# Phase 1's weight pieces: 512 columns in place of 256, one begun every fourth tile

## Chip, cores and metric

The kernel runs on one core of one Trainium2 chip. The metric is the device time of one execution in microseconds, the median of several runs. The engines are named as in the profile: PE (TensorE matmuls), PEld (its weight loads), DVE (VectorE), ACT (ScalarE), POOL (GpSimd), SP (SyncE, which here issues all DMAs).

## What is computed

Attention with a threshold under each row's maximum, then two feed-forward layers on the 2304 tokens:

```python
batch, n_heads, seq, head_dim = (4, 8, 576, 64)
scores = scale * np.matmul(q, k.transpose(0, 1, 3, 2))
thresh = np.max(scores, axis=-1, keepdims=True) - tau
scores = np.where(scores >= thresh, scores, -1000000000.0)
scores = scores - np.max(scores, axis=-1, keepdims=True)
attn = np.exp(scores)
attn = attn / (np.sum(attn, axis=-1, keepdims=True) + 1e-09)
x = np.matmul(attn, v)            # to 2304 tokens of 512
...
g = x @ w_gate                    # 512 to 1536
silu = g * (1.0 / (1.0 + np.exp(-g)))
x = silu * (x @ w_val) @ w_out    # 1536 to 512
...
h = np.maximum(x @ w_in, 0.0)     # 512 to 2048
return h * h @ w_out2             # 2048 to 512
```

The weights come in as float64 (the products of a float32 draw and a float64 scalar); the kernel converts them itself.

## The kernel before

Each matrix product of the feed-forward layers is made of three TensorE products of a rounded part (hi, FP32r) and a remainder (lo): hi by hi, hi by lo, lo by hi. So every operand is split: ACT copies with rounding (`ops.copy`, L48), and DVE or POOL subtracts (`ops.sub`, L56).

*Phase 1* runs attention in 144 tiles of 128 queries (4 batches, 4 pairs of heads, 9 tiles each; the fifth of the nine has queries of both heads). Per tile: `QK` (PE, L583), `RED` the row maximum (DVE, L595), `EXP` (ACT, L601) and the threshold (L603), `MASK` (DVE, L612), `RCP` (L618), `NORM` (POOL, L623), `TR` five transposes (PE, L643), copies of these into `ptf` or `pt`, `AV` the product with the values (PE, L699 in batch 0, L702 later), and the copy of its result into `xF` (ACT L48; DVE L714 adds the second half). Two score buffers, three buffers for `e`. Per pair of heads a load (L424) and small moves (L524), all on SP's one queue.

When a batch is done, its tokens go through the first group of the first feed-forward layer, five slices of 128 hidden columns, as *fill* between attention's tiles: for each half batch `stage_x` splits `xF` into `xs_m`, then per slice gate and value (L220) and, after the five, the output product (`out1`, L265). `work` hands out fill by a credit per tile (`rate`). Batches 0 to 2 are done so; the rest is *phase 2*, which has only feed-forward layers.

*The weights' loader.* `Loader` brings float64 weights in pieces of `PIECE` = 256 columns: one DMA on SP (L122), then seven steps: absolute value of the high words (ACT, L131), four integer steps (DVE: L133 and L135 with one tensor in, L139 and L141 with two, one of them the raw words), the rounded copy (ACT, L48) and the remainder (POOL in phase 1, DVE in phase 2, L56). In phase 1 the raw words and most of the working columns lie in parts of `xF` of the last batch, which nothing uses yet; there are `LIVE` = 3 such buffers. Phase 1 needs 7680 columns, 30 pieces: first those of gate and value by slice, then those of w_out.

What sets the order: in the main loop over tiles `loader.start` is called every `cfg["lev"]` = 2 tiles from tile 8 on, and begins a piece if fewer than `cfg["live"][0]` = 3 have steps ahead of their sixth. `loader.tick(engine)` (named LD, LA, LP) lets the first piece that may go on do one step on that engine; a step on another engine than the last needs a newer `age`, and only `start` advances `age`. `loader.until(f, col)` runs starts and ticks in a loop until slice f is converted up to a column; the fill calls it ahead of each slice. Then a list scheduler places every instruction on its engine's queue by priority (program order with the offsets of `cfg["early0"]` and `cfg["early"]`) and by what it depends on; each engine works its queue in order. The scheduler sees dependences of two accesses by the stretch of memory that each covers.

## Time and profile before

| | us |
|---|---|
| median of 3 runs (1180.57 to 1181.55) | 1181.24 |
| profiled execution | 1181.87 |
| its span, first to last instruction | 1179.8 |
| PE busy | 1142.7 (97%) |
| DVE busy | 874.8 (74%) |
| ACT busy | 647.2 (55%) |
| POOL busy | 294.4 (25%) |

The shares are means over stages of different kinds: POOL works only in phase 1, which ends at about 467 us. So the rows below are by stretch. The profiled execution lies 2.1 us above its span, and 0.6 us above the median.

### The profile page before, as it was taken

How to read it: one execution, taken by the hardware profiler on the slowest of the kernel's cores; microseconds unless marked ns; L12 is line 12 of the kernel's file. 1: busy time of each engine (PE TensorE's matmuls, PEld its weight loads, DVE VectorE, ACT ScalarE, POOL GpSimd, SP SyncE). 2: the span in 40 equal slices, each digit the busy share in tenths (PEclk: the TensorE clock that was granted, in tenths of full speed). 3: DMA queues.
4: the chain of work that ended last, by engine and by line, in shares of the span. 5: the costliest groups of instructions: out<-in, count | busy, mean ns of one | idle time of the engine just before them, and what ended most of it. 6: DMA issues, size and time to landing. Idle time of an engine off the chain costs nothing.

```text
span 1179.8 us, 19121 instructions
## 1 busy us (share of the span) xinstructions
PE 1142.7 (97%) x6564; PEld 1010.0 (86%) x6564; DVE 874.8 (74%) x2058; ACT 647.2 (55%) x1552; POOL 294.4 (25%) x421
## 2 busy tenths in 40 slices
PE   5888899999999999999999999999999999999998
PEld 4677889999999999998888888888888888888887
DVE  6989996799989994789985863468458858755533
ACT  5878888888777774454442432245455525433321
POOL 4556775777766653000000000000000000000000
PEclk9999999999999999999999999999999999999999
DMA  5666533444343310232320210002102101100111
GB/s 170 167 175 177 148 91 81 100 117 106 91 104 94 97 32 1 81 100 80 88 65 8 83 54 1 1 27 67 50 19 71 55 19 36 55 1 1 45 58 59
DMA packets 40848, 84.73 MB, mean 72 GB/s; under 512 B 5936, under 2 KB 6960, under 8 KB 40752
## 3 DMA queue, kind: packets, MB, share of 16 engines
q1 hardware_dynamic: 40752, 83.52, 25.2%
q8 instruction: 52, 0.85, 0.3%
q14 instruction: 44, 0.36, 0.1%
HBM read 52.23 MB, written 4.72 MB: 48 GB/s over the span
## 4 chain that ended last, share of the span: by engine, by line
PE 81%; DVE 11%; issue 3%; ACT 2%; DMA 1%; POOL 1%; SPq 0%; POOLq 0%; DVEq 0%; ACTq 0%
PE mm L220 34%; PE mm L311 17%; PE mm L265 9%; PE s L583 4%; PE bank L220 4%; PE bank L643 4%; PE bank L265 4%; PE bank L702 3%; DVE e L612 3%; DVE nm L595 2%; PE bank L699 1%; DVE xs_m L56 1%; DMA xF<-in_w_dram 1%; DVE pt L56 1%; DVE xF L714 1%
## 5 line engine op out<-in xcount | busy, mean ns | idle before, releaser
L220 PE MATMUL mm<-xs,wa 128*128 128x512 f32 (+2 forms) x1152 | 226.3, 356 | 0.5 <-ACT x L48 0.5
L220 PEld LDWEIGHTS mm<-xs,wa 128*128 128x128 f32 x1152 | 193.4, 188 | 30.9 <-ACT x L48 0.7
L220 PE MATMUL mm<-xs,wb 128*128 128x512 f32 (+1 forms) x840 | 175.5, 368 | 0.0
L643 PE MATMUL bank<-ident,e 128*128 128x128 f32 x720 | 163.6, 276 | 6.9 <-ACT x L48 3.6
L220 PEld LDWEIGHTS mm<-xs,wb 128*128 128x128 f32 x840 | 146.8, 188 | 26.4
L623 POOL TENSOR_SCALAR e<-e,r 128x576 f32<-128x576 f32 x144 | 113.9, 792 | 87.0 <-DVE r L618 39.2
L612 DVE SCALAR_TENSOR_TENSOR e<-s,thr,e 128x577 f32<-128x577 f32 x144 | 116.8, 812 | 14.7 <-ACT e L601 11.0
L595 DVE TENSOR_REDUCE nm<-s 128x1 f32<-128x576 f32 x144 | 108.0, 751 | 7.7 <-PE s L583 6.8
L663 ACT ACTIVATE pt<-bank 128x384 fp32r<-128x384 f32 (+1 forms) x216 | 92.2, 437 | 38.5 <-PE bank L643 33.2
L220 PE MATMUL bank<-xs_m,wa 128*128 128x288 f32 x576 | 109.7, 326 | 3.0 <-DVE xs_m L56 1.9
L601 ACT ACTIVATE e<-s,nm 128x576 f32<-128x576 f32 x144 | 107.1, 744 | 7.2 <-DVE nm L595 3.9
L643 PEld LDWEIGHTS bank<-ident,e 128*128 128x128 f32 x720 | 97.4, 142 | 15.7 <-POOL e L623 4.9
L294 ACT ACTIVATE k_th<-mm 128x512 f32<-128x512 f32 (+1 forms) x80 | 43.7, 547 | 120.0 <-PE mm L220 118.9
L583 PE MATMUL s<-kh,qs 128*128 128x288 f32 x256 | 80.7, 329 | 16.2 <-DVE e L612 8.8
L702 PE MATMUL bank<-pt,vs 128*128 128x256 f32 (+1 forms) x480 | 92.9, 321 | 2.2 <-POOL pt L56 1.5
L220 PEld LDWEIGHTS bank<-xs_m,wa 128*128 128x128 f32 x576 | 89.0, 189 | 5.8 <-DVE xs_m L56 3.3
L295 DVE TENSOR_TENSOR k_th<-k_th 128x512 f32<-128x512 f32 (+1 forms) x80 | 50.7, 634 | 52.6 <-ACT k_th L294 52.0
L131 ACT ACTIVATE wf<-wr 128x256 f32<-128x256 f32 x106 | 45.5, 433 | 72.3 <-DMA wr<-in_w_dram 57.1
L702 PEld LDWEIGHTS bank<-pt,vs 128*128 128x128 f32 x480 | 73.6, 189 | 4.3 <-POOL pt L56 2.8
L324 DVE TENSOR_TENSOR xF<-xF,mm 128x512 f32<-128x512 f32 x54 | 37.0, 684 | 54.2 <-PE mm L311 54.2
L583 PE MATMUL s<-kl,qs 128*128 128x288 f32 x256 | 73.9, 302 | 0.0
L583 PEld LDWEIGHTS s<-kh,qs 128*128 128x128 f32 x256 | 49.5, 194 | 22.4 <-DVE e L612 13.3
(125 smaller groups left out, 2280.4 us busy)
## 6 DMA issues: line engine op xcount, KB each, us to landing
wr<-in_w_dram SPq DMA_DIRECT2D x106, 256.0 KB, 3.0
raw<-in_qkv_dram SPq DMA_DIRECT2D x15, 896.0 KB, 4.6
kh<-land SPq DMA_DIRECT2D x60, 144.0 KB, 2.5
kl<-raw SPq DMA_DIRECT2D x60, 144.0 KB, 2.7
xF<-in_w_dram SPq DMA_DIRECT2D x30, 256.0 KB, 3.1
out_dram<-xF SPq DMA_DIRECT2D x18, 256.0 KB, 2.0
qs<-land SPq DMA_DIRECT2D x30, 144.0 KB, 2.5
qs<-raw SPq DMA_DIRECT2D x30, 144.0 KB, 2.6
```

Of the source, the lines that this page charges most:

```text
L220: mm(pt[:, :n], w[:, a, col + c * P : col + (c + 1) * P], xs[:, b, c, :], start=(i == 0), stop=(i == len(TERMS) - 1),)
L265: mm(pt[:, :n], w[:, a, 2 * DM + m * P : 2 * DM + (m + 1) * P], u[:, b, :], start=(k == 0), stop=(k == last),)
L295: ("D", lambda: nc.vector.tensor_tensor(th, th, th, op=ALU.mult)),
L311: mm(pt, u[:, b, s * P : (s + 1) * P], w[:, a, DM : 2 * DM], start=(k == 0), stop=(k == last),)
L583: mm(sp[:, cols], l, r[:, cols], start=(n_ == 0), stop=(n_ == len(pairs) - 1),)
L595: nc.vector.tensor_reduce(nm, sv, axis=AX.X, op=ALU.max, negate=True)
L601: nc.scalar.activation(e[:, :S], st[t]["s"][:, :S], AF.Exp, bias=st[t]["nm"])
L612: nc.vector.scalar_tensor_tensor(e, st[t]["s"][:, : S + 1], st[t]["thr"], e, op0=ALU.is_ge, op1=ALU.mult, accum_out=sum_)
L623: nc.gpsimd.tensor_scalar(e, e, scalar1=r, scalar2=1.0, op0=ALU.mult, op1=ALU.mult)
L643: mm(dst[:, j], e[:, c0 : c0 + P], ident, is_transpose=True, start=(j == 0), stop=(j == len(cols) - 1),)
L663: nc.scalar.activation(pt[:, s0 : s0 + n, o : o + P], src, AF.Copy)
L702: mm(o[:, :n], hd["vs"][:, SLOT[k % 5], :], pt[:, k, lo : lo + n], start=(k == 0), stop=(k == 9))
```

## The change

In phase 1 a piece has 512 columns, 15 pieces in place of 30. `PIECE` is now a pair, one size for each phase; phase 2 keeps 256 columns, and its loads and steps cover the same memory as before. There are two buffers for three: the raw words lie in two row blocks of `xF`, the last batch's first 512 columns of each (`two` gives loads and steps two rows of half a piece), the working columns in the third batch's part. `start` is called every fourth tile (`lev` 4), two pieces are live at once, and two of the four calls of `tick` for DVE are gone from the loop. An assertion says that the loader is done before batch 2 writes its part.

```diff
--- before.py
+++ after.py
@@ -29,8 +29,8 @@
 G2 = [4, 4, 4, 4]
 NBS = [(0, 512), (512, 512), (1024, 512), (1536, 512), (2048, 256)]
 NB = 512
-PIECE = 256
-LIVE = 3
+
+PIECE = (512, 256)
 VW = 5 * D
 RAWW = 2 * S + 2 * VW
 
@@ -108,24 +108,25 @@
 
         def add(self, src, f, width, area, k):
             w = area[:, k * 2 * width : (k + 1) * 2 * width].rearrange("p (a c) -> p a c", a=2)
-            self.todo += [(src, f, w, c0) for c0 in range(0, width, PIECE)]
+            self.todo += [(src, f, w, c0, PIECE[self.phase]) for c0 in range(0, width, PIECE[self.phase])]
             return w
 
         def start(self):
             self.age += 1
             if not self.todo or sum(x[2] < 6 for x in self.live) >= cfg["live"][self.phase]:
                 return
-            src, f, w, c0 = self.todo.pop(0)
+            src, f, w, c0, n = self.todo.pop(0)
             self.n += 1
-            sl = slice(c0, c0 + PIECE)
+            sl = slice(c0, c0 + n)
             raw, fl = self.bufs[self.n % len(self.bufs)]
-            nc.sync.dma_start(raw, src[f, :, sl])
-            g = self.steps(raw, fl, w[:, 0, sl], w[:, 1, sl], self.n)
+            two = lambda x: x.rearrange("p (a n) -> p a n", a=2)
+            nc.sync.dma_start(raw.bitcast(I64), two(src[f, :, sl]))
+            g = self.steps(raw, two(fl), two(w[:, 0, sl]), two(w[:, 1, sl]), self.n)
             self.live.append([g, next(g), 1, "S", self.age, (f, c0)])
 
         def steps(self, raw, fl, whi, wlo, n):
-            words = raw.bitcast(I32).rearrange("p (n two) -> p n two", two=2)
-            lo, hi = words[:, :, 0], words[:, :, 1]
+            words = raw.bitcast(I32).rearrange("p a (n two) -> p a n two", two=2)
+            lo, hi = words[:, :, :, 0], words[:, :, :, 1]
             yield "A"
             it = fl.bitcast(I32)
             nc.scalar.activation(fl, hi.bitcast(F32), AF.Abs)
@@ -382,10 +383,8 @@
     up = p1.enter_context(tc.tile_pool(name="up", bufs=1))
     xsp = p1.enter_context(tc.tile_pool(name="xsp", bufs=1))
 
-    for j in range(LIVE):
-        c0 = LAST + j * PIECE
-        fl = xF[:, LIVE, c0 : c0 + PIECE] if c0 + PIECE <= NT else up.tile([P, PIECE], F32, name=f"wf{j}")
-        loader.bufs.append((xF[:, j, LAST : LAST + 2 * PIECE].bitcast(I64), fl))
+    for j in range(2):
+        loader.bufs.append((xF[:, 2 * j : 2 * j + 2, LAST : LAST + PIECE[0]], xF[:, j, LAST - S : LAST - S + PIECE[0]]))
     psum = p1.enter_context(tc.tile_pool(name="psum", bufs=1, space=PSUM))
     bank = [psum.tile([P, 512], F32, name=f"bank{j}") for j in range(4)]
     mp1 = Mm(bank[3:])
@@ -704,6 +703,8 @@
         out_x = [(xF[mr, p, base + dst : base + dst + w], slice(src, src + w)) for dst, src, w in segs]
 
         def main():
+
+            assert b < 2 or not loader.todo and not loader.live
             for x_, sl in out_x:
                 ops.copy("A" if not one else cfg["om"], x_, o[mr, sl])
             if one:
@@ -839,7 +840,6 @@
         if 0 <= i - 1 < NTILE:
             at_(RCP, i - 1)
             at_(NORM, i - 1)
-        at_(loader.tick, "D", name="LD")
         at_(mp1.flush, "A", name="FA")
         if i + 1 < NTILE:
             at_(QK, i + 1)
@@ -862,7 +862,6 @@
                 if k == 2:
                     steps = pair_steps(pr + 1)
                 at_(next, steps, name="PS")
-        at_(loader.tick, "D", name="LD")
     while avq or not fstate["end"]:
         mp1.age += 1
         mp1.flush()
@@ -894,7 +893,7 @@
 
     wrp = p2.enter_context(tc.tile_pool(name="wrp", bufs=1))
     loader.bufs = [
-        (wrp.tile([P, PIECE], I64, name=f"wr{j}"), wrp.tile([P, PIECE], F32, name=f"wf2{j}")) for j in range(2)
+        (wrp.tile([P, 2, PIECE[1]], F32, name=f"wr{j}"), wrp.tile([P, PIECE[1]], F32, name=f"wf2{j}")) for j in range(2)
     ]
     wts[0] = W
     loader.phase = 1
@@ -1045,7 +1044,7 @@
     "qs": "A",
     "thr": "A",
     "wl": "PD",
-    "live": (3, 2),
+    "live": (2, 2),
     "fill": 6,
     "om": "A",
     "early0": {
@@ -1053,7 +1052,7 @@
         "RED": -12, "RCP": 4, "MASK": 4, "NEG": -60,
     },
     "three": 20,
-    "lev": 2,
+    "lev": 4,
     "ldat": 8,
     "early": {
         "TR": 8, "LD": -21, "FD": 4, "NEG": -4, "FA": -19, "PL": -12, "PS": -25, "PH": 6, "LS": 64, "RCP": -8,
```

The first place is DVE's queue around tiles 9 and 10 (`nm9` is the row maximum of tile 9, `wf` and `xF` are pieces' working columns). Before:

```order
L595 TENSOR_REDUCE nm9_373<-s1_110 128x1
L141 SCALAR_TENSOR_TENSOR xF_64<-xF_64 128x256
L133 TENSOR_SCALAR wf2_80<-wf2_80 128x256
L595 TENSOR_REDUCE nm10_410<-s0_109 128x1
L612 SCALAR_TENSOR_TENSOR e0_97,sum9_405<-s1_110,thr9_374,e0_97 128x577
L135 TENSOR_SCALAR wf2_80<-wf2_80 128x256
L618 RECIPROCAL r9_406<-sum9_405 128x1
L139 SCALAR_TENSOR_TENSOR wf2_80<-xF_64,wf2_80 128x256
L141 SCALAR_TENSOR_TENSOR wf2_80<-xF_64,wf2_80 128x256
L612 SCALAR_TENSOR_TENSOR e1_98,sum10_430<-s0_109,thr10_411,e1_98 128x577
L618 RECIPROCAL r10_431<-sum10_430 128x1
```

Now:

```order
L594 TENSOR_REDUCE nm9_372<-s1_109 128x1
L617 RECIPROCAL r8_368<-sum8_367 128x1
L594 TENSOR_REDUCE nm10_408<-s0_108 128x1
L611 SCALAR_TENSOR_TENSOR e0_96,sum9_403<-s1_109,thr9_373,e0_96 128x577
L617 RECIPROCAL r9_404<-sum9_403 128x1
L611 SCALAR_TENSOR_TENSOR e1_97,sum10_427<-s0_108,thr10_409,e1_97 128x577
L617 RECIPROCAL r10_428<-sum10_427 128x1
L594 TENSOR_REDUCE nm11_432<-s1_109 128x1
L594 TENSOR_REDUCE nm12_462<-s0_108 128x1
```

The steps of pieces have left this place: the next one after tile 5 stands behind the row maximum of tile 15.

The second place is where the fill's first output product stands, PE's queue behind the scores of tile 59 before and of tile 61 now (`m00_2_u` is the hidden slice 2, `bank3` and `bank2` are accumulators). Before:

```order
L583 MATMUL s1_110<-kl13_2142,qs13_2140 128x288
L702 MATMUL bank2_86<-pt_132,vs12_2092 128x256 x10
L265 MATMUL bank3_87<-m00_0_u_1351,wa_69 128x288 x3
L265 MATMUL bank3_87<-m00_1_u_1451,wa_69 128x288 x3
L265 MATMUL bank3_87<-m00_2_u_1596,wa_69 128x288
L643 MATMUL bank0_84<-ident_113,e2_99 128x128
L265 MATMUL bank3_87<-m00_2_u_1596,wa_69 128x288
L643 MATMUL bank0_84<-ident_113,e2_99 128x128
```

Now:

```order
L582 MATMUL s1_109<-kl13_2049,qs13_2047 128x288
L266 MATMUL bank3_86<-m00_2_u_1519,wa_69 128x288 x3
L266 MATMUL bank3_86<-m00_3_u_1681,wa_69 128x288 x3
L701 MATMUL bank2_85<-pt_131,vs11_1629 128x256 x8
L266 MATMUL bank3_86<-m00_4_u_1826,wx_73 128x288 x2
L701 MATMUL bank2_85<-pt_131,vs11_1629 128x256
L266 MATMUL bank3_86<-m00_4_u_1826,wx_73 128x288
L701 MATMUL bank2_85<-pt_131,vs11_1629 128x256
L672 MATMUL bank0_83<-pt_131,nident_117 128x384
L672 MATMUL bank1_84<-pt_131,nident_117 128x256
L266 MATMUL bank3_86<-m00_0_u_1272,wa_69 128x288 x3
```

Before, transposes of attention stand between the output's matmuls, and tile 60's scores follow; now the whole first output product and value products of earlier tiles stand in a row, and tile 62's scores behind them. On DVE there, before:

```order
L612 SCALAR_TENSOR_TENSOR e2_99,sum59_2432<-s1_110,thr59_2396,e2_99 128x577
L595 TENSOR_REDUCE nm60_2439<-s0_109 128x1
L618 RECIPROCAL r59_2433<-sum59_2432 128x1
L56 TENSOR_TENSOR pt_132<-bank1_85,pt_132 128x2x128
L595 TENSOR_REDUCE nm61_2480<-s1_110 128x1
L612 SCALAR_TENSOR_TENSOR e0_97,sum60_2473<-s0_109,thr60_2440,e0_97 128x577
L618 RECIPROCAL r60_2474<-sum60_2473 128x1
L56 TENSOR_TENSOR pt_132<-bank0_84,pt_132 128x3x128
```

and now:

```order
L594 TENSOR_REDUCE nm61_2359<-s1_109 128x1
L134 TENSOR_SCALAR xF_64<-xF_64 128x512
L136 TENSOR_SCALAR xF_64<-xF_64 128x512
L140 SCALAR_TENSOR_TENSOR xF_64<-xF_64 128x512
L142 SCALAR_TENSOR_TENSOR xF_64<-xF_64 128x512
L134 TENSOR_SCALAR xF_64<-xF_64 128x512
L715 TENSOR_TENSOR xF_64<-xF_64,bank2_85 64x256
L136 TENSOR_SCALAR xF_64<-xF_64 128x512
L140 SCALAR_TENSOR_TENSOR xF_64<-xF_64 128x512
L142 SCALAR_TENSOR_TENSOR xF_64<-xF_64 128x512
L715 TENSOR_TENSOR xF_64<-xF_64,bank2_85 64x256 x2
```

The two last pieces are converted between the row maximum of tile 61 and the mask of tile 60.

The third place is ACT's queue with the semaphores that its instructions wait for (DMAHW: a DMA's; the others an engine's), near tile 23 before and near tile 31 now, where `xF` is staged into `xs_m` and an attention output goes into `xF`. Before:

```order
L603 ACTIVATE thr22_779<-nm22_778,tau_n_61 128x1
L603 ACTIVATE thr23_812<-nm23_811,tau_n_61 128x1 [waits DVE_49]
L131 ACTIVATE wf2_80<-xF_64 128x256 [waits DMAHW5_49,Pool_49]
L48 ACTIVATE xs_m00_1341<-xF_64 128x288
L601 ACTIVATE e2_99<-s1_110,nm23_811 128x576 [waits PE_49]
L48 ACTIVATE x2_65<-bank1_85 128x2x128
L48 ACTIVATE xF_64<-bank2_86 64x256 [waits PE_49]
```

Now:

```order
L48 ACTIVATE xs_m00_1262<-xF_64 128x288 [waits DMAHW3_49]
L48 ACTIVATE xs_m00_1262<-xF_64 128x288 [waits Activation_49]
L48 ACTIVATE x2_65<-bank0_83 128x3x128 [waits PE_49]
L600 ACTIVATE e1_97<-s1_109,nm31_1007 128x576 [waits DVE_49,PE_49,Pool_49]
L602 ACTIVATE thr31_1008<-nm31_1007,tau_n_61 128x1
L48 ACTIVATE x2_65<-bank1_84 128x2x128
L602 ACTIVATE thr32_1037<-nm32_1036,tau_n_61 128x1 [waits DVE_49]
L600 ACTIVATE e2_98<-s0_108,nm32_1036 128x576 [waits PE_49,Pool_49]
L48 ACTIVATE x2_65<-bank1_84 128x2x128
L48 ACTIVATE xF_64<-bank2_85 64x256 [waits DMAHW1_49,PE_49]
L48 ACTIVATE x2_65<-bank0_83 128x3x128 [waits DVE_49,PE_49]
```

One staging copy and one output copy now wait for a DMA; before neither did.

## Rows read from the trace of the kernel before

**Rows 1.** Busy us by stretch: PE, PEld, DVE, ACT, POOL, then PEclk, DMA, GB/s

```profile
11.40:110.20 98.80, 84.62 (x466) 69.28 (x466) 90.23 (x230) 78.07 (x200) 53.35 (x73) 0.98 0.58 153
110.20:166.30 56.10, 50.41 (x349) 45.66 (x348) 54.81 (x129) 47.03 (x125) 40.47 (x54) 1.00 0.52 139
166.30:195.50 29.20, 28.48 (x209) 26.93 (x209) 22.61 (x55) 23.37 (x62) 18.33 (x26) 1.00 0.38 94
195.50:200.70 5.20, 5.20 (x43) 5.20 (x42) 3.27 (x10) 4.13 (x12) 2.46 (x3) 1.00 0.00 0
200.70:467.50 266.80, 263.90 (x2001) 257.48 (x2001) 233.12 (x570) 204.04 (x524) 173.66 (x245) 1.00 0.35 85
467.50:1179.80 712.30, 707.80 (x3498) 603.50 (x3497) 467.64 (x1063) 287.17 (x628) 0.98 (x2) 1.00 0.14 46
```

**Rows 2.** Line 595 by stretch: count, ns min/median/max, first and last start, shapes

```profile
L595 DVE TENSOR_REDUCE nm<-s x9: 742/757/758, 11.4 to 30.2; 128x1 f32<-128x576 f32 x9
...
L595 DVE TENSOR_REDUCE nm<-s x37: 730/745/758, 11.4 to 110.2; 128x1 f32<-128x576 f32 x37
...
L595 DVE TENSOR_REDUCE nm<-s x16: 737/746/757, 110.2 to 164.2; 128x1 f32<-128x576 f32 x16
...
L595 DVE TENSOR_REDUCE nm<-s x8: 745/752/760, 166.3 to 190.9; 128x1 f32<-128x576 f32 x8
...
L595 DVE TENSOR_REDUCE nm<-s x10: 745/752/760, 166.3 to 198.0; 128x1 f32<-128x576 f32 x10
```

**Rows 3.** DVE groups, 520 to 1179 us: count, busy us, mean ns, idle before

```profile
L295 DVE TENSOR_TENSOR k_th<-k_th 128x512 f32<-128x512 f32 x64 | 44.0, 687 | 40.1 <-ACT k_th L294 39.5
...
L141 DVE SCALAR_TENSOR_TENSOR wf<-wr,wf 128x256 int32<-128x256 int32 x91 | 38.4, 421 | 1.8
...
L135 DVE TENSOR_SCALAR wf<-wf 128x256 int32<-128x256 int32 x91 | 26.4, 290 | 1.9
```

**Rows 4.** Timeline of DVE at 57 us: start, duration, instruction

```profile
57.14 0.29 DVE L135 TENSOR_SCALAR xF<-xF 128x256 int32<-128x256 int32 x1
57.34 0.88 DVE L141 SCALAR_TENSOR_TENSOR wf<-xF,wf 128x256 int32<-128x256 int32 x1
```

**Rows 5.** DVE groups, 11.4 to 110.2 us, then 110.2 to 166.3 us

```profile
L139 DVE SCALAR_TENSOR_TENSOR xF<-xF 128x256 int32<-128x256 int32 x13 | 6.2, 485 | 0.0
...
L535 DVE SCALAR_TENSOR_TENSOR raw<-raw,qscale,land 128x576 fp32r<-128x576 f32 x4 | 4.0, 998 | 2.0 <-ACT land L529 2.0
...
L135 DVE TENSOR_SCALAR wf<-wf 128x256 int32<-128x256 int32 x6 | 2.4, 392 | 0.0
...
L135 DVE TENSOR_SCALAR xF<-xF 128x256 int32<-128x256 int32 x7 | 4.2, 605 | 0.1
...
L133 DVE TENSOR_SCALAR wf<-wf 128x256 f32<-128x256 f32 x4 | 1.6, 398 | 0.0
```

**Rows 6.** Timeline of DVE and of POOL at 139 us

```profile
139.37 0.97 DVE L139 SCALAR_TENSOR_TENSOR xF<-xF 128x256 int32<-128x256 int32 x1
...
139.26 0.81 POOL L56 TENSOR_TENSOR m_u<-m_th,m_u 128x288 fp32r<-128x288 f32 x1
```

**Rows 7.** Line 122, the weights' loads

```profile
DMA to landing us min/median/max: 2.5/3.0/7.5
```

**Rows 8.** Groups: ACT, 520 to 1179 us; POOL, 11.4 to 200.7 us

```profile
L48 ACT ACTIVATE ub<-k_th 128x512 fp32r<-128x512 f32 x47 | 29.6, 630 | 28.6 <-DVE k_th L295 17.4 <-DVE k_th L250 10.9
...
L56 POOL TENSOR_TENSOR wa<-xF,wa 128x256 fp32r<-128x256 f32 x17 | 12.9, 766 | 4.7 <-ACT wa L48 4.6
...
L56 POOL TENSOR_TENSOR pt<-tf,pt 128x384 fp32r<-128x384 f32 x5 | 5.1, 1012 | 0.2 <-ACT tf L666 0.2
```

**Rows 9.** The chain that ended last, at 190 us: start, us, what

```profile
190.36 1.19 PE bank L702 x10
191.55 0.93 PE bank L265 x7
```

**Rows 10.** Timeline of PE at 96 us

```profile
96.64 0.71 PE L643 MATMUL bank<-ident,e 128*128 128x128 f32 x5
```

## The prediction

> **What bounds the kernel now.** I read four views in this order: busy time by stretch, the groups of VectorE's (DVE's) instructions, the timeline, the chain of work. By stretch [rows 1] TensorE (PE) is busy for 707.8 of 712.3 us after 467.5, and for 263.9 of 266.8 us between 200.7 and 467.5. The built order of phase 2 is the same in both kernels, and that of phase 1 is the same on every engine from about tile 62 on. So from 200.7 us on a change in the start time is carried to the end one to one, and all is decided ahead of that. There attention's tiles are counted by their row maximum (L595) [rows 2]: tiles 0 to 35 take 11.4 to 110.2 us (stretch A), 36 to 51 to 166.3 (B), 52 to 61 to 200.7 (C). In A and B DVE is the busiest engine, 90.2 of 98.8 and 54.8 of 56.1 us. In C PE is: 28.5 of 29.2, then 5.2 of 5.2. The weights' conversion is what loads DVE in A and B and is nearly absent in C.
>
> **Price of one conversion instruction on DVE.** A piece has four: two with one SBUF tensor in (L133, L135), two with two (L139, L141). Alone (late in the program, where GpSimd does nothing) they last 290 and 421 ns at 256 columns [rows 3]. At 512 columns an instruction with two inputs lasts 687 ns [rows 3]. One with a single input and 512 columns isn't in the trace: between 290 (no dearer) and 580 (twice); I take 420, since 256 columns add 267 ns with two inputs and the single-input form is faster per column. An instruction begins some 0.08 us before the record of the one ahead of it ends: one of 0.29 us at 57.14 is followed at 57.34 [rows 4]. So one costs on average (290+421)/2 - 80 = 275 ns of DVE's time at 256 columns and (420+687)/2 - 80 = 473 ns at 512.
>
> In A and B they are dearer. In A the eight groups hold 75 instructions and 33.2 us, 443 ns each; in B 43 and 23.4 us, 544 ns each (first and last group in [rows 5]): 0.09 and 0.19 us above the 355 ns alone. The surplus is a collision: at 139.37 an L139 took 0.97 us and ended 0.27 us after the GpSimd instruction that began at 139.26 and lasted 0.81 [rows 6]. I take the surplus per instruction, not per column, as it ends with the other engine's instruction: 0.56 us each in A, 0.66 in B and C. The Trainium skill's page SBUF — State Buffer (Who interferes with whom) says that the two engines' shared port pair is an exclusive lock, held for a whole instruction. By that rule half as many instructions meet half as many locks, and the row agrees.
>
> **Part by part.** The built order tells where the 60 instructions (15 pieces by four) that replace 120 stand: 16 in A, 23 in B, 21 in C; before it was 75, 43 and 2. Pieces are not only wider but later: the hand-over of a piece from one engine to the next needs a newer `age`, which only `start` advances, and that is now called every fourth tile; and only two are begun at a time. Before the fill's weights are used, `until` then forces what is missing.
>
> *A.* DVE loses 75 x 0.36 = 27.2 us and gets 16 x 0.56 = 9.0: -18.2. Then PE (84.6 busy) and ScalarE (78.1, of which some 8 goes too) are late next, so the gain lies between 0 and 18.2. The nearest row is the pace of the first eight tiles, 11.4 to 30.2 [rows 2]: 2.35 us each, with seven 256-wide conversions among them, some 2 us, which is 9 us in 36 tiles, just what is left in A. 36 x 2.35 = 84.6: **-14.2**.
>
> *B.* 43 x 0.46 - 23 x 0.66 = -4.7 on DVE. PE, at 50.4 busy of 56.1, leaves room for that, but the conversions now come in bursts: between -4.7 and +2 (a burst of four at 0.66 that nothing covers), I take **-3.5**.
>
> *New waits.* The raw buffer was one run of columns in one row block of `xF`; now it is a block of two, and what lies between them counts as covered. In the built order a staging copy of `xF` (L48, into xs_m) and a copy of an attention output into `xF` wait for a DMA's semaphore; before none did. Behind such a copy on ScalarE stands the next tile's exp. A load of 256 KB lands 3.0 us after its issue, at most 7.5 [rows 7]; it is 512 KB now. Two such waits stand on ScalarE late in A, one on DVE there and one on DVE in C: 0 if the load is early, up to some 6 us; **+2**. SP's queue gets 15 loads for 30, each waiting for a buffer that frees two pieces earlier; the pair's moves behind them are asked for no earlier than by the order, so I cost them at nothing; an uncovered wait is like the 2.0 us that L535 waited in A [rows 5].
>
> *C.* The three last pieces (columns of w_out) are converted here, after the tiles 52 to 55 have run without any fill. In tiles 52 to 59 DVE had 22.6 us of work in 29.2; 13 conversions at 0.66 (8.6) replace two (0.6): 30.6, about 1 us more than now. Then, at tile 61, DVE does the last two pieces in a row, and PE's queue holds the five w_out groups that read them. From the end of piece 12: two row maxima (0.75 each), piece 13's four steps (1.9), a wait for piece 14's load (some 1), its four (1.9), ScalarE's rounding (0.63), GpSimd's remainder; that is 766 ns at 256 columns and 1012 at 384, so some 1.25 at 512 [rows 8]: 8 us, in which PE has four scores (0.5), two groups (0.8) and eight value matmuls (1.0). After it PE has 37 matmuls of the output, 12 of the next gate, ten value matmuls, ten transposes: 49 x 0.131 + 1.2 + 1.4 + 0.5 = 9.5 [rows 9, 10]. 17.5 us in place of 5.2: +12.3. With the 1 us it is 13.3 at most; if ScalarE and GpSimd are quicker to turn, or PE takes up the value matmuls earlier, half of the 8 us is hidden, so between +7 and +16; I take **+12**. The Trainium skill (Perfetto Trace Analysis, Optimizing Scalar/DVE Operations) says that where Scalar and Vector aren't saturated but hold others up, smaller instructions let work be done sooner. In C that speaks against this change; split in 256 columns, each of the last chain's steps would hand over its first half sooner, by some 2 us in all, an estimate.
>
> Sum: -14.2 - 3.5 + 2 + 12 = -3.7. On the profiled execution of 1181.87 us it gives 1178.2; the median of the runs is 0.6 lower, so **1178 us**. A measurement of this kernel can tell some 0.2% (2.4 us) from no change.
>
> **Rivals.**
> - *The starved fill wins (slower).* If C and the new waits together cost more than the 17.7 us that A and B give, the kernel is slower. With C at +16, the waits at +5 and A at -12, B at -3: +6, 1187 us. For it: PE has no fill for four tiles, and every wait in C falls on the engine that sets the end there [rows 1]. Against it: PE's work up to tile 62 is the same, and A has 14.2 us of idle PE.
> - *The burst hides (much faster).* A falls by 17, C costs 7: -12, 1169 us. For it: DVE is idle for 8.5 us of C now. Against it: PE's queue is in order, and the value matmuls stand behind the output's.
> - *Wide instructions collide in proportion.* If the surplus grows with the columns, B and C's price is 0.473 x 0.464/0.275 = 0.80 us, 0.14 more for 44: +6 on the forecast, 1183 to 1184 us, so little or nothing is left. Against it is [rows 6].
>
> **How the numbers follow.** Forecast 0.40 (of it 0.27 faster by over 0.2%, 0.13 within); starved fill 0.33 (0.30 slower, 0.03 within); hidden burst 0.13; proportional collisions 0.14 (0.09 within, 0.05 slower). Faster 0.40, within 0.25, slower 0.35. The forecast's own range is 1174 to 1182. For 8 in 10 it reaches into both neighbours: A -18 and C +9 give 1168, A -7, C +14 and the waits +4 give 1190.
>
> **What would show it.** Right: tile 36's row maximum begins by about 96 us, DVE's L140/L142 last about 0.69 us where GpSimd is idle, and tile 62's comes at about 197, after a gap of some 17 us from tile 60's. From there to the end both traces take the same 979 us. Wrong: a pace in A that stays near 2.7 us a tile; PE idle at the output's matmuls for much more or less than 6 us; ScalarE waiting for DMAs ahead of xs_m.

## The result

| | before | after |
|---|---|---|
| median of 4 runs each, us | 1180.99 (1180.57 to 1181.55) | 1192.66 (1191.65 to 1196.66) |
| ratio, 95% interval | | 1.0113 (1.0099 to 1.0126) |
| profiled execution, its span | 1181.87, 1179.8 | 1196.66, 1194.9 |
| tile 0's row maximum begins | 11.4 | 9.9 |
| tile 36's | 110.2 | 101.6 |
| tile 52's | 166.3 | 154.8 |
| tile 60's | 195.5 | 190.5 |
| tile 62's | 200.7 | 215.4 |

The change made the kernel 11.7 us slower, where 1178 us (1168 to 1190) was forecast. The profiled execution is the slowest of its four, 4.0 us above their median, so what it shows is larger by that than the usual run; the seventh experiment shows where most of those 4 us may lie.

Busy time by stretch, cut at the same tiles as [rows 1] (PE, PEld, DVE, ACT, POOL, then PEclk, DMA share, GB/s):

```profile
9.90:101.60 91.70, 82.56 (x465) 68.72 (x466) 74.07 (x171) 70.96 (x171) 45.76 (x61) 0.96 0.57 151
101.60:154.80 53.20, 49.25 (x346) 45.05 (x345) 49.23 (x106) 45.11 (x114) 40.40 (x47) 1.00 0.54 143
154.80:190.50 35.70, 25.16 (x148) 20.89 (x147) 29.42 (x63) 23.64 (x59) 21.65 (x26) 0.93 0.45 121
190.50:215.40 24.90, 19.59 (x108) 17.52 (x108) 10.87 (x21) 10.68 (x25) 7.65 (x8) 0.68 0.07 21
215.40:482.50 267.10, 264.06 (x2000) 257.54 (x1999) 233.16 (x570) 203.96 (x524) 173.30 (x245) 1.00 0.35 85
482.50:1194.90 712.40, 707.77 (x3499) 603.93 (x3497) 467.22 (x1063) 287.49 (x628) 1.07 (x2) 1.00 0.15 46
```

From tile 62 on the two traces last 979.1 (before) and 979.5 us (after). Ahead of it, the changed kernel is 11.6 us early at tile 52 (A gave 8.6, B 3.0) and 14.7 us late at tile 62. So ten tiles, stretch C, took 60.6 us in place of 34.4: 26.2 us lost, against 12 in the forecast. In C no engine is full now: PE is busy for 44.8 of 60.6 us, DVE for 40.3. And the column PEclk says 0.93 and 0.68 where [rows 1] have 1.00.

### The profile page after: what moved, and what is told of

Same layout as the page of the kernel before. It is cut to its first block, busy times and chain, and to the rows that moved or that the text cites. A ratio compares the mean times of both kernels' runs of the same rounds, so it can differ in the third digit from the quotient of the medians.

```text
span 1194.9 us, 19005 instructions
## 1 busy us (share of the span) xinstructions
PE 1150.7 (96%) x6564; PEld 1015.6 (85%) x6564; DVE 866.8 (73%) x1998; ACT 644.8 (54%) x1522; POOL 293.6 (25%) x406
## 4 chain that ended last, share of the span: by engine, by line
PE 83%; DVE 7%; ACT 3%; DMA 3%; issue 2%; POOL 2%; SPq 0%; POOLq 0%; DVEq 0%; ACTq 0%
PE mm L221 34%; PE mm L312 16%; PE mm L266 9%; PE bank L221 5%; PE s L582 5%; PE bank L642 4%; PE bank L266 4%; PE bank L701 4%; PE bank L698 2%; DVE e L611 2%; DMA xF<-in_w_dram 1%; DVE nm L594 1%; DMA raw<-in_qkv_dram 1%; DVE pt L56 1%; ACT e L600 1%
## 5 line engine op out<-in xcount | busy, mean ns | idle before, releaser
L221 PEld LDWEIGHTS mm<-xs,wa 128*128 128x128 f32 x1152 | 193.5, 189 | 30.8 <-ACT x L48 0.7
L642 PE MATMUL bank<-ident,e 128*128 128x128 f32 x720 | 159.2, 278 | 10.6 <-ACT x L48 3.7
L296 DVE TENSOR_TENSOR k_th<-k_th 128x512 f32<-128x512 f32 (+1 forms) x80 | 50.8, 635 | 51.3 <-ACT k_th L295 50.8
L132 ACT ACTIVATE wf<-wr 128x256 f32<-128x256 f32 x106 | 45.4, 432 | 71.2 <-DMA wr<-in_w_dram 62.9
L325 DVE TENSOR_TENSOR xF<-xF,mm 128x512 f32<-128x512 f32 x54 | 37.0, 686 | 53.7 <-PE mm L312 53.7
```

What stands on the lines that cost most here:

```text
L221: mm(pt[:, :n], w[:, a, col + c * P : col + (c + 1) * P], xs[:, b, c, :], start=(i == 0), stop=(i == len(TERMS) - 1),)
L296: ("D", lambda: nc.vector.tensor_tensor(th, th, th, op=ALU.mult)),
L642: mm(dst[:, j], e[:, c0 : c0 + P], ident, is_transpose=True, start=(j == 0), stop=(j == len(cols) - 1),)
```

## The experiments

Each kernel ran beside the kernel before. "Conversions" are DVE's instructions of pieces in A, B and C as the built order has them; tile 36 is the time of its row maximum, B and C the lengths of tiles 36 to 51 and 52 to 61, all from the profiled execution.

| kernel | conversions | tile 36 | B | C | median us | ratio (95%) |
|---|---|---|---|---|---|---|
| before | 75, 43, 2 | 110.2 | 56.1 | 34.4 | 1180.99 | |
| after | 16, 23, 21 | 101.6 | 53.2 | 60.6 | 1192.66 | 1.0113 |
| 1: one row block | 41, 19, 0 | 105.8 | 52.2 | 34.9 | 1176.16 | 0.9961 (0.9946, 0.9975) |
| 2: start every 2nd tile | 34, 22, 4 | 105.9 | 59.2 | 36.1 | 1182.34 | 1.0019 (1.0007, 1.0030) |
| 3: before, in two row blocks | 65, 31, 24 | 106.5 | 58.7 | 50.8 | 1197.60 | 1.0145 (1.0120, 1.0170) |
| 4: 1 and 2 together | 47, 13, 0 | 107.2 | 51.2 | 34.9 | 1173.02 | 0.9933 (0.9914, 0.9952) |
| 5: working columns moved out | 24, 20, 16 | 103.8 | 53.7 | 45.3 | 1186.61 | 1.0051 (1.0035, 1.0067) |
| 6: before, start every 4th | 69, 44, 7 | 108.5 | 57.4 | 35.5 | 1182.86 | 1.0026 (1.0015, 1.0037) |
| 7: extra matmuls | 16, 23, 21 | 97.9 | 53.0 | 60.0 | 1194.02 | 1.0116 (1.0101, 1.0131) |
| 8: three buffers | 49, 11, 0 | 109.5 | 53.2 | 34.9 | 1178.59 | 0.9986 (0.9975, 0.9996) |
| 9: 5 and 2 together | 38, 22, 0 | 109.1 | 55.6 | 33.0 | 1178.05 | 0.9984 (0.9972, 0.9995) |
| 10: 4, first start at tile 4 | 47, 13, 0 | 111.1 | 50.6 | 34.8 | 1177.98 | 0.9984 (0.9973, 0.9996) |
| 11: 1, start every 3rd tile | 45, 15, 0 | 107.2 | 51.0 | 34.8 | 1176.06 | 0.9964 (0.9950, 0.9979) |
| 12: 4 again | 47, 13, 0 | 107.7 | 50.8 | 34.8 | 1172.72 | 0.9924 (0.9910, 0.9938) |

(Where an expectation below names other counts by a few, the table's are right.)

Two theories stood against each other on why the pieces come so late. *Pace*: a start only every fourth tile and two live pieces, as the prediction had it. *Block shape*: the raw words now lie in two row blocks of `xF`, and the scheduler takes such a block as one stretch of memory, from the first row block's last batch to the second's. All of the second row block's earlier columns lie in it: attention's results of batches 0 to 2, what `stage_x` reads, and, for the first buffer, the second buffer's working columns.

**1. One row block.** Same width, same starts; only where the buffers lie.

```diff
-        loader.bufs.append((xF[:, 2 * j : 2 * j + 2, LAST : LAST + PIECE[0]], xF[:, j, LAST - S : LAST - S + PIECE[0]]))
+        r0 = LAST - S
+        loader.bufs.append(
+            (
+                xF[:, j, r0 : r0 + 2 * PIECE[0]].rearrange("p (a n) -> p a n", a=2),
+                xF[:, 2 + j, r0 : r0 + PIECE[0]],
+            )
+        )
```

> The changed kernel with the raw words of a piece in one row block of xF (1024 columns, from the third batch's part on) and the working columns in the two row blocks behind; a start still stands at every fourth tile, two pieces live, 512 columns. Theory 'block shape' (the two-row block counts as covering what lies between its two parts, so a piece cannot be placed ahead of attention's copies into xF): all 60 conversions now stand ahead of tile 52 (41 in A, 19 in B), tiles 52 to 61 take 34 us as in the kernel before and the gain of A and B stays: 8 to 10 us, 1169 to 1174 us. Theory 'pace' (every fourth tile and two live make the pieces late): C keeps some 20 of its 26 us, 1185 us or more.

Stretches A, B and C (to tile 60, then to 62), columns as above:

```profile
9.50:105.80 96.30, 80.81 (x466) 65.96 (x466) 86.87 (x194) 77.15 (x184) 54.67 (x66) 1.00 0.62 172
105.80:158.00 52.20, 49.33 (x344) 45.17 (x344) 47.76 (x105) 44.24 (x112) 39.63 (x48) 1.00 0.51 135
158.00:187.60 29.60, 28.85 (x213) 27.47 (x212) 22.46 (x53) 23.84 (x63) 16.86 (x25) 1.00 0.38 92
187.60:192.90 5.30, 5.30 (x43) 5.30 (x43) 3.29 (x11) 4.29 (x12) 2.51 (x4) 1.00 0.00 0
```

C is back at 34.9 us with PE full, and the clock at 1.00 throughout. 1176.16 us: 16.5 less than after, with the pace untouched. So the pace alone doesn't make the pieces late. (In columns it had not changed: 512 every fourth tile for 256 every second.)

**2. A start every second tile**, the two-row block kept.

```diff
-    "lev": 4,
+    "lev": 2,
```

> The changed kernel with a start every second tile in place of every fourth; two-row blocks stay. In its order 34 conversions stand in A, 22 in B, 4 in C. Both theories expect C near 34 to 38 us. 'Block shape' expects that waits for DMAs on ScalarE stay, so some 2 us more than with one block: 1171 to 1177 us. 'Pace' expects all the loss to go, as with nothing else wrong: 1169 to 1172 us.

C is nearly restored (36.1), yet the time is 1182.34: B takes 59.2 us, 3.1 more than before, though DVE is busy for 49.4 us of it in place of 54.8. Twice the columns per tile nearly undo the lateness, but not the other costs of the block. PE's clock falls too, to a mean of 0.97 in B and 0.95 in C. What ScalarE, and then GpSimd, waited for (us in total, times, longest):

```profile
ACT xF L132 <- POOL wa L56: 6.4, 5, 3.2
...
ACT xF L132 <- POOL wx L56: 1.5, 1, 1.5
```

```profile
POOL wa L56 <- DMA xF<-in_w_dram: 2.7, 3, 1.5
```

GpSimd's wait is the mark of the block. Its remainder reads a piece's working columns and its rounded part, no raw words; here it waits for a *load* of raw words. That is the next piece's load into the first buffer, in whose stretch the second buffer's working columns lie. ScalarE's `L132` of a later piece waits for that remainder, and attention's copies and exp stand behind it. The longest of ScalarE's waits (3.2 us, at 151) isn't explained by that alone: GpSimd did other work there and waited for no load, with the remainder late in its queue. That the block put it there is likely, since none of these waits is left in experiment 9, but not shown; experiment 6, without such a block, has a wait of this kind of 3.1 us.

**3. The kernel before, in two row blocks.** 256 columns, three live, a start every second tile as before; only the buffers' places differ: two raw buffers of three are folded, the third lies elsewhere in one row block, and the first buffer's working columns lie in the second's stretch, as a neighbour's do in the changed kernel (in that kernel's writing, with `PIECE` = (256, 256), the two ticks back):

```diff
...
-        loader.bufs.append((xF[:, j, LAST : LAST + 2 * PIECE].bitcast(I64), fl))
...
+        r0, c0 = ((0, LAST), (2, LAST), (0, LAST + PIECE[0]))[j]
+        fl = (xF[:, 2, LAST + 256 : LAST + 512], xF[:, 3, LAST + 256 : LAST + 512], None)[j]
...
+        raw = xF[:, r0 : r0 + 2, c0 : c0 + 256]
+        if j == 2:
+            raw = xF[:, 2, LAST - S : LAST - S + 512].rearrange("p (a n) -> p a n", a=2)
+        loader.bufs.append((raw, fl))
```

> The kernel before with 256 columns, a start every second tile and three live as it was, but two of the three raw buffers laid over two row blocks (256 columns of each) and the third in one row block elsewhere. 'Block shape': pieces are late again (24 conversions in C, output products in a lump behind tile 61 in its order), C takes 15 to 25 us more, A and B lose up to 5: 1190 to 1205 us. 'Pace': 1180 to 1184 us, since the pace is that of before.

1197.60 us, 17 more than before: the block, with a neighbour's columns in it, lengthens C at 256 columns and the old pace too, by 16.4 us. With experiment 1 this is the cause from both sides.

**4 and 12. One row block and a start every second tile**, both edits above in one kernel.

> One row block and a start every second tile: 47 conversions in A, 12 in B and 1 in C's first tile, none in the rest. If DVE's saved time in A and B is what is left, it stands within 3 us of the run with one block and every fourth tile; earlier pieces put 6 more of them into A (some 3 us of DVE there) and 7 fewer into B: 1168 to 1175 us. If late pieces were still costing something in the run with one block, this one is the faster by over 2 us.

> The kernel with one row block and a start every second tile once more, on another chip's time and in five rounds, since the four kernels with one row block lay between 1173.0 and 1178.0. If its gain is the build's (no wait of ScalarE for GpSimd ahead of L132, PE without a fall of its clock in A): 1172 to 1175 us again. If the first 1173.0 was a lucky draw among falls of the clock in A: 1175 to 1178 us.

1173.02 and, some time later, 1172.72 us: 0.7% under the kernel before, the best of all, and it came out twice.

**5. The working columns out of the block.** Raw words stay in two row blocks; the second buffer's working columns go from row block 1 to row block 2, ahead of the second buffer's stretch.

```diff
-xF[:, j, LAST - S : LAST - S + PIECE[0]]
+xF[:, 2 * j, LAST - S : LAST - S + PIECE[0]]
```

> The changed kernel, raw words still in two row blocks and a start every fourth tile, but the second buffer's working columns moved from row block 1 to row block 2: out of the stretch that the first buffer's raw words count as covering. In its order C holds 16 conversions in place of 21, the last behind tile 57 in place of 61, and 22 in A in place of 16. Theory 'pieces hold each other up' (the second buffer's columns lie inside the first's block): most of C's loss goes, 1178 to 1184 us. Theory 'attention's copies hold pieces up' (the blocks cover columns that copies and staging touch): C keeps over half of its 26 us, 1187 to 1193 us.

Tiles 52 to 59 and 60 to 61:

```profile
157.50:197.00 39.50, 32.33 (x207) 29.17 (x207) 31.84 (x70) 27.57 (x71) 25.62 (x30) 0.91 0.41 112
197.00:202.80 5.80, 5.80 (x47) 5.80 (x46) 3.28 (x8) 4.41 (x12) 2.17 (x4) 1.00 0.00 0
```

The second part of C is normal (5.8 us), the first takes 39.5 in place of 29.2. C is 15.3 us shorter than in after and still 10.9 longer than before. So pieces holding each other up are a real part of the loss, and what the fold still covers, attention's copies and staging, is the likely rest. How large each is stays open: the two profiles say 15.3 of 26.2 us of C, but after's lies 4.0 us above its median and this one 3.0 below; the medians say 6.1 (1186.61 for 1192.66) of the 16.5 that one row block gives. The time lies between the two expectations.

**6. The pace alone.** The kernel before with `"lev": 4`.

> The kernel before with one number changed: a start every fourth tile in place of every second (256 columns, one row block each, three live). In its order 89 conversions stand in A and the first eighth of B... 69 in A, 44 in B, 7 in C (75, 43 and 2 before). Theory 'pace': pieces come half as often, the fill starves, 1190 us or more. Theory 'block shape': the scheduler places forced pieces early enough when nothing in memory speaks against it; C costs 3 us more at most: 1179 to 1184 us.

1182.86 us, +0.26%. At half the pace in columns, with one row block, the pieces still come early: 7 conversions in C, C 1.1 us longer.

**7. Extra matmuls in the waits.** The changed kernel with matmuls of a zero tile in the first output product's accumulation.

```diff
...
+                extra = warm.get((nm, m, k // 3), 0)
+                for i in range(extra):
+                    mm(pt[:, :n], zero, us[-1][:, 0, :], start=(k + i == 0), stop=False)
...
```

> The changed kernel with 48 extra matmuls of a zero weight tile (16 ahead of the first output product, 24 ahead of its fourth slice, 8 ahead of its fifth), which add zero; 6.3 us of PE at the full clock. They stand on PE where it waited between 184 and 197 us. Theory 'clock' (some 4 to 6 us of C are PE's work at half its clock after those waits): the granted clock stays near 1.0 in more of 180 to 206 us, tile 62 comes no later than in the changed kernel and up to 4 us earlier, 1188 to 1193 us. Theory 'waits alone': the clock is no cause, and what of the 6.3 us doesn't fit into the waits is added: 1193 to 1199 us.

A, B, C to tile 60, and to 62:

```profile
9.70:97.90 88.20, 79.39 (x465) 66.41 (x466) 74.18 (x172) 71.02 (x171) 46.04 (x61) 1.00 0.59 159
97.90:150.90 53.00, 49.21 (x346) 44.93 (x345) 49.22 (x105) 45.11 (x114) 40.35 (x47) 1.00 0.54 143
150.90:193.40 42.50, 33.29 (x191) 28.76 (x190) 33.78 (x69) 26.12 (x63) 23.70 (x29) 0.88 0.41 114
193.40:210.90 17.50, 15.79 (x113) 14.64 (x112) 6.81 (x15) 8.17 (x21) 5.60 (x7) 1.00 0.00 1
```

As to the time it is inconclusive: 1194.02 is after's within the intervals. In C the end ran at 1.00 in place of 0.68 and took 17.5 us in place of 24.9, while the first part took 6.8 us longer: the 48 extra matmuls were busy for 8.3 us, 12 of them at the low clock, and 40 of them stand in that part. So the extra work was about paid back. But on PE and on DVE some other instructions of C stand in another order too, so what the clock alone is worth there isn't shown.

A tells more. Up to tile 56 every engine's order is that of the changed kernel, apart from the zero tile's one memset, and here A ends at 97.9 with the clock at 1.00, there at 101.6 with 0.96. Counted from tile 0 (9.7 and 9.9) that is 3.5 us, most of what the profiled execution of after lies above its median; whether its other runs lack them isn't shown (their mean clocks are 0.990 to 0.992, this one's 0.989). By tile 25's row maximum 1.4 of the 3.5 are lost, mostly behind loads that land later; the other 2.2 come by tile 27, where PE works at the low clock.

**8. Three buffers, three live**, one row block, a start every second tile: the starts and live pieces of before, at 512 columns (the two calls of `tick` stay out).

```diff
+    for j in range(3):
+        r0 = LAST - S
+        fl = xF[:, 3, r0 + j * PIECE[0] : r0 + (j + 1) * PIECE[0]] if j < 2 else up.tile([P, PIECE[0]], F32, name="wf")
+        loader.bufs.append((xF[:, j, r0 : r0 + 2 * PIECE[0]].rearrange("p (a n) -> p a n", a=2), fl))
...
```

> 512 columns with all else of the pace as in the kernel before: one row block of raw words, three buffers, three live, a start every second tile (two calls of tick less). 49 conversions in A, 11 in B, none in C. This is the width alone. Half as many instructions on DVE at 0.53 to 0.73 us in place of 0.37 to 0.49 us: some 20 us less of DVE's time in A and B, of which PE's work lets 7 to 10 us through: 1171 to 1174 us. If the third buffer is worth something it is below the run with two buffers (1173.0) by over 1 us.

1178.59, not 1171 to 1174. C is right; A and B are each 2.0 us longer than in experiment 4, B at the full clock and for a reason left open. In A ScalarE waits at 96.86 for GpSimd's remainder of a piece, and PE, which then waits for 1.5 us at 97.5 and 1.1 at 101.0, works at the low clock behind that (stretches from 98 us, PE's busy time first, its clock third from the end):

```profile
96.86 0.69 ACT L132 ACTIVATE xF<-xF 128x512 f32<-128x512 f32 x1 [1.96 <-POOL wx L56]
```

```profile
98.00:100.00 2.00, 0.83 (x5) 1.00 0.81 202
100.00:106.20 6.20, 5.15 (x20) 0.60 0.07 28
```

Nine runs of ten show a mean clock of 0.997 or less here, those of experiment 4 show 0.999 or 1.0. More pieces under way do not help here; in this place one piece's abs stands on ScalarE ahead of a remainder that GpSimd hasn't done.

**9. 5 and 2 together.**

> Raw words in two row blocks, the second buffer's working columns in row block 2, and a start every second tile. In its order 38 conversions in A, 22 in B, none in C: so the lateness is gone, and of the two-row block only the dependence on attention's copies and staging is left. Theory 'what is left of the block costs nothing once the pieces are early': as with one row block and a start every second tile, 1172 to 1175 us. Theory 'attention's copies still cost': as with the columns inside and a start every second tile, 1179 to 1183 us. ScalarE's wait for GpSimd ahead of L132 (7.9 us in A and B with the columns inside, none with one block) shows which of the two it is.

1178.05: 4.3 less than with the columns inside, 5.0 more than with one row block. ScalarE's wait for GpSimd is gone, as is GpSimd's for a load. What is left of the loss is in A (99.3 us at a clock of 0.97, 97.8 at 1.00 in experiment 4) and B; which dependence makes it isn't shown. The time lies between the two expectations.

**10 and 11. Variations of one row block**: the first start at tile 4, and a start every third tile.

> One row block, a start every second tile, the first at tile 4 in place of 8: 8 conversions ahead of tile 8 in place of 5, 47 in A as before, 12 in B, 1 behind. DVE is idle for some 2 us ahead of tile 8, so up to 2 us less than the run with the first start at tile 8 (1173.0): 1171 to 1174 us. If the loads, which come amid the first pair's, hold up attention's first moves, up to 3 us more.

> One row block and a start every third tile: 45 conversions in A, 15 in B, none in C. Between the runs with every second (1173.0) and every fourth (1176.2) if the pace as such matters: 1173 to 1176 us. If it does not, their difference is the clock's falls in A, and this one may lie anywhere from 1171 to 1178 us, with the granted clock below 1 in A where it is slow.

1177.98 and 1176.06. In the tenth the piece's loads go out ahead of one of the first pair's loads (L465), which goes out at 8.49 where experiment 4 issues its last at 5.43; tile 0 starts at 11.4 in place of 9.5, 1.9 us of the 4.9 between the two medians. A is 1.9 us longer too, at the full clock, and why is open. SP's rows:

```profile
4.48 0.91 SPq L123 DMA_DIRECT2D xF<-in_w_dram  x2
...
8.49 0.43 SPq L465 DMA_DIRECT2D x<-in_qkv_dram  x1
```

The eleventh has the same span as experiments 1 and 4 in the profile (1172.4, 1171.9, 1172.3), but its runs spread from 1173.9 to 1178.3, with clocks from 0.997 to 1.0. Of experiment 1's six runs the profiled one took 1173.67 at a mean clock of 1.0, and the five others 1175.8 to 1177.0 at 0.998; all nine runs of experiments 4 and 12 took at most 1174.6 at 0.999 or 1.0. So these kernels with a start every second tile are some 3 us better than experiment 1, and the difference goes with a lower clock in experiment 1's usual runs. ScalarE's wait for GpSimd ahead of `L132` may be why, since experiments 1 (1.6 us at 98) and 11 have it and 4 doesn't; but no trace here shows a slower run, and the eleventh's clocks don't sort its times.

## Why the prediction was wrong

The profiled execution missed the forecast by some 18 us (1196.7 for 1178.2): C by 14.2, A by 5.6, B by 0.5, less the 2 that were put down to waits apart. The two times named as signs did not come: tile 36 began at 101.6, not by 96, and tile 62 at 215.4, not at 197.

**What bounds: right.** From tile 62 on both traces take 979 us, and the start time was carried to the end.

**Price of an instruction: right.** Conversions of 512 columns in B, where GpSimd is busiest:

```profile
L140 DVE SCALAR_TENSOR_TENSOR xF<-xF 128x512 int32<-128x512 int32 x6 | 5.1, 854 | 0.0
L142 DVE SCALAR_TENSOR_TENSOR xF<-xF 128x512 int32<-128x512 int32 x5 | 4.5, 901 | 0.0
L134 DVE TENSOR_SCALAR xF<-xF 128x512 f32<-128x512 f32 x6 | 4.4, 740 | 0.0
L136 DVE TENSOR_SCALAR xF<-xF 128x512 int32<-128x512 int32 x6 | 3.9, 648 | 0.1
```

Where GpSimd was idle they lasted 0.42 to 0.43 (L134, L136) and 0.69 us (L140, L142), as taken. In B the 23 hold 17.9 us, 0.78 each, 0.22 above that; at 256 columns it was 0.19 [rows 3, 5]. Had the surplus grown with the columns, 0.33 would stand there. The page SBUF — State Buffer of the Trainium skill (Who interferes with whom) has the lock held for a whole instruction, and this agrees; that rival was rightly put low.

**B: right** (-3.0, forecast -3.5). **A: right in kind, too large, and missing a term**: -8.6 for -14.2, of it -1.6 already at tile 0, which the sum didn't have. In the seventh experiment the same order gave -12.3, so even at the full clock A itself is 88.2 us for the 84.6 of the sum; what held the rest isn't shown. The 3.7 us between the two runs are 0.2 at tile 0, 1.4 mostly behind loads that land later, and 2.2 behind a fall of the clock at 70 us. The chain begins with the new block. SP issues a piece's load at 62.3, GpSimd's remainder of another piece waits until it lands, ScalarE's `L132` for that remainder, and behind it stands the copy out of PSUM that PE's next transposes wait for; PE idles for 2.2 us, then works at 1.2 GHz (rows of SP, GpSimd, ScalarE and PE, then the stretches 68 to 72 and 72 to 76 us, PE's busy time first, its clock third from the end):

```profile
62.32 0.53 SPq L123 DMA_DIRECT2D xF<-in_w_dram  x1
```

```profile
67.42 1.27 POOL L56 TENSOR_TENSOR wa<-xF,wa 128x512 fp32r<-128x512 f32 x1 [2.95 <-DMA xF<-in_w_dram]
```

```profile
68.72 0.68 ACT L132 ACTIVATE xF<-xF 128x512 f32<-128x512 f32 x1 [2.19 <-POOL wa L56]
69.30 0.48 ACT L48 ACTIVATE x<-bank 128x384 f32<-128x384 f32 x1
```

```profile
69.92 2.31 PE L642 MATMUL bank<-ident,e 128*128 128x128 f32 x7 [2.20 <-ACT x L48]
```

```profile
68.00:72.00 4.00, 1.96 (x7) 0.71 0.15 40
72.00:76.00 4.00, 4.00 (x13) 0.50 0.22 48
```

In the second stretch PE is busy throughout and has 13 matmuls, where the seventh experiment at the full clock has 23 in its 72 to 76. That experiment has the same chain, but there the load lands after 4.3 us for 5.0 here, PE idles for less, and the clock stays:

```profile
68.39 0.52 PE L648 MATMUL bank<-ident,e 128*128 128x128 f32 x3 [1.47 <-ACT x L48]
```

**New waits (+2): the wrong engines.** I read from the built order that staging and output copies wait for a DMA, and priced these. None of the copies waited for a load in the trace of after (in experiment 3 one staging copy did, for 0.9 us). The waits that came stand on a piece's own steps which read no raw words: GpSimd's remainder (2.9 us, once) and DVE's L134 (2.5 us, twice). Such waits appear in every kernel with working columns inside the block (after, 2, 3, 7), and none of 0.4 us or more in the others.

**The reason for the lateness: wrong.** "Pieces are not only wider but later: the hand-over needs a newer `age`" named the pace. The counts per stretch came from the built order, so the sum didn't suffer, but the reading did: experiments 1, 3 and 6 show the block's shape and place; the pace only sets how far it shows (experiment 2). I had seen the two-row stretch and took it only for a source of waits; it also bars the scheduler from moving pieces ahead, past each other and, as experiment 5 suggests, past attention's copies.

**C (+12): the step that failed.** The mechanism, two pieces converted in a row at tile 61 with PE's queue held behind them, was there, and its size was off by 14 us (26.2):

- *Tiles 52 to 59*, +1 forecast, +6.5 measured. I compared DVE's work with the stretch, 30.6 of it (29.4 measured). But with the fill gone PE was busy for 25.2 of 35.7 us and DVE for 29.4, the clock was 0.93, and no engine's sum set the time: it was the chain of attention's tiles, one step after another. An engine's sum is a bound only where something else fills the waits.
- *Tiles 60 and 61*, +12.3 forecast, +19.7 measured. The chain of 8 us from piece 12's end to piece 14's remainder took 11.7 (190.6 to 202.3). DVE's rows, from ahead of tile 60:

```profile
187.04 0.43 DVE L134 TENSOR_SCALAR xF<-xF 128x512 f32<-128x512 f32 x1 [1.73 <-DMA xF<-in_w_dram]
187.38 0.81 DVE L611 SCALAR_TENSOR_TENSOR e<-s,thr,e 128x577 f32<-128x577 f32 x1
...
191.43 0.76 DVE L594 TENSOR_REDUCE nm<-s 128x1 f32<-128x576 f32 x1
192.10 0.81 DVE L134 TENSOR_SCALAR xF<-xF 128x512 f32<-128x512 f32 x1
192.94 0.85 DVE L136 TENSOR_SCALAR xF<-xF 128x512 int32<-128x512 int32 x1
195.09 0.69 DVE L140 SCALAR_TENSOR_TENSOR xF<-xF 128x512 int32<-128x512 int32 x1 [1.29 <-ACT xF L132]
195.81 0.69 DVE L142 SCALAR_TENSOR_TENSOR xF<-xF 128x512 int32<-128x512 int32 x1
196.54 0.43 DVE L134 TENSOR_SCALAR xF<-xF 128x512 f32<-128x512 f32 x1
...
197.44 1.36 DVE L136 TENSOR_SCALAR xF<-xF 128x512 int32<-128x512 int32 x1
198.84 0.69 DVE L140 SCALAR_TENSOR_TENSOR xF<-xF 128x512 int32<-128x512 int32 x1
199.56 0.69 DVE L142 SCALAR_TENSOR_TENSOR xF<-xF 128x512 int32<-128x512 int32 x1
```

L140 of piece 13 waits 1.29 us for piece 14's abs on ScalarE, a false wait of the same kind, since nothing of piece 13 needs it (the sum had some 1 us of wait for that load). Three of the single-input steps, beside GpSimd's work (191.4 to 193.5 and 197.3 to 198.5), took 0.81, 0.85 and 1.36 in place of 0.42. PE's rows, and its clock by stretch:

```profile
188.26 0.40 PE L582 MATMUL s<-kh,qs 128*128 128x288 f32 x1 [2.03 <-DVE e L611]
...
190.06 0.61 PE L582 MATMUL s<-kh,qs 128*128 128x288 f32 x1 [1.01 <-DVE e L611]
...
197.22 0.85 PE L266 MATMUL bank<-m_u,wa 128*128 128x288 f32 x2 [3.93 <-ACT wa L48]
...
202.32 0.61 PE L266 MATMUL bank<-m_u,wx 128*128 128x288 f32 x1 [0.29 <-POOL wx L56]
...
203.48 3.06 PE L266 MATMUL bank<-m_u,wa 128*128 128x288 f32 x12
...
207.97 1.75 PE L266 MATMUL bank<-m_u,wa 128*128 128x288 f32 x12
...
214.66 0.29 PE L582 MATMUL s<-kh,qs 128*128 128x288 f32 x1
```

```profile
184.00:189.00 5.00, 2.11 (x12) 1.00 0.65 183
189.00:197.00 8.00, 2.78 (x8) 0.51 0.23 66
197.00:206.00 9.00, 7.90 (x29) 0.50 0.00 0
206.00:215.40 9.40, 9.40 (x74) 0.99 0.00 0
```

PE idled for 2.9 us of 184 to 189, and its clock then stayed at 1.2 GHz to 206 us. Of the 2.9, 2.0 end with the mask of 187.38, which follows ScalarE's exp (186.3 to 187.1) and DVE's `L134` of piece 12. That `L134` had waited 1.7 us for piece 13's load, a false wait of the block, and the piece's other steps and tile 60's row maximum stand behind it; how much of the 1.7 reached PE isn't shown. The low clock shows in the matmuls: 12 matmuls of the output took 3.06 us at 203 and 1.75 at 208. From 197 to 206 PE was busy for 7.9 us at half its clock, 3.95 us that I had priced at the full one. The Trainium skill's page TensorE: Matmul & The Clock Gate (HAM oscillation) reckons the extra time of a low stretch as its length times one minus 1.2/2.4; by that it would be 4.5 of the 9 us, and the row's busy time makes it 3.95. No term of my sum had the clock in it, although the kernel before shows a fall too, at 72 to 80 us of its A (0.82 and 0.75 in four-us stretches).

**The rivals.** The starved fill was the one that came, with 0.33. Its price of +6 took C at +16 and waits at +5, where C alone was +26; the range ended at 1190 because each bound of C was still one at the full clock. (With B and the waits as in the sum, the terms named for the range's ends give 1171 and 1189; the result lies outside either way.) The burst that hides (1169) failed as it was said it would: PE's queue is in order, and PE had nothing else.

## What to carry to other kernels

A wide buffer that is folded over two rows costs what the scheduler thinks lies between the rows: look at what the stretch covers before looking at what the change saves, and at a buffer's neighbour among the pieces first. When a change takes an in-order PE's other work away, price the following work at the clock that a wait leaves, and price the stretch by its chain, not by its busiest engine's sum. What the width alone is worth is open: with one row block and starts every second tile, 512 columns gave 0.7% with two pieces live, and 0.1% with three as before; 256 columns with two live were not run.

## What the runs showed of the hardware

A single-input DVE instruction of 512 columns in SBUF (L134 on floats, L136 on integers) lasts 0.42 to 0.44 us where one of 256 lasts 0.29: doubling the width costs 0.13 us there and 0.27 with two inputs. Beside a GpSimd instruction three such single-input ones took 0.81, 0.85 and 1.36 us. One fall of TensorE's clock, right behind a wait of 2.2 us on PE, cost 2.2 us in A for the same instructions; behind a wait of 1.5 us in the same place it didn't come. In C it stayed at the low level for 17 us, from 189 to 206, through further waits, and came back after nine us in which PE was busy for 7.9.
